# A loop of small matmuls on TensorE during the modulation, and the first gate load as one transfer

## The chip, the core and the metric

The kernel runs on one core of a Trainium2 chip. Its time is the device time of that core in microseconds (us), and less is better. All input weights and caches lie in HBM and are read once.

## What is computed

The reference is one decode step of a transformer block with adaptive layer norm, for 8 sequences of one token, in bf16, cut here to what matters:

```python
mod = (silu(c) @ w_mod).reshape(8, 6, 1, 1024)          # six modulation vectors
sa, ca, ga, sb, cb, gb = (mod[:, i] for i in range(6))
h = layernorm(x) * (1 + ca) + sa
q = h @ wq                                              # 32 heads of 128
p = softmax(q @ k_cache.T * 128 ** -0.5)                # 4 kv heads, 8192 keys each
x = x + ga * ((p @ v_cache) @ wo)
h = layernorm(x) * (1 + cb) + sb
gate, up = h @ W_gate, h @ W_up                         # 1024 to 3584
x = x + gb * ((relu(gate) * up) @ W_down)
```

`w_mod` is 1024 x 6144, `k_cache` and `v_cache` are 8 x 4 x 8192 x 128. With the weights that is 185.6 MB to read.

## The kernel before

Every operation is first entered in a graph (`g.op`), which adds a wait for each read or write that another engine has to finish first; each engine then runs its own list in the order in which it was entered. All matmuls go through the helpers `mm` (line 304) and `tr` (line 308, a transpose), all VectorE operations through line 312, and ScalarE's through line 315. These helpers are the lines that the profile names.

**The stream.** All weights and caches come through one buffer, `ring`, of 11 x 8192 bf16 columns on 128 partitions. The list `stream` fixes the order of the blocks: four of `w_mod` (3 MB each), four of `wq` (2 MB), then the k and v blocks of the 32 pairs of sequence and kv head (2 MB each, `k` ahead of `v` by two), four of `wo` among them, then gate and up in turns (four of each, 1.75 MB), and five of `W_down`, the last two of 0.5 MB. SyncE's queue (SP) issues all of these loads (line 630). A load waits only for the last matmul that used the piece of the ring which it overwrites. `pieces()` says how many transfers a block is cut into: one for all blocks but `("gate", 0)`, which goes as eleven: its second half of 3584 columns, columns 256 to 3583 of its first half, and the first 256 columns in nine transfers of 1, 2, 3, 4, 5, 6, 7, 4 and 96 partitions.

**The stages.** The modulation is a loop of eight `k` over four blocks, with 12 matmuls of 512 columns in each `k`:

```python
for k in range(KD):
    w = place[("mod", k // 2)][:, k % 2, :]
    for f in range(12):
        j, q = f // 4, f % 4
        mm(mbank[j][0][32 * q:32 * q + B, :], siluT[:, k, :], w[:, 512 * f:512 * (f + 1)], ...)
```

Its three PSUM banks are copied out, transposed and added up to `modT`, and `hT` is made of it. The matmuls with `wq` follow (64 of them, on `hT`), then q is laid out, and the attention loop begins: for each of the 32 pairs 64 transposes of the k block on TensorE, copies of them by VectorE and ScalarE, scores, softmax and the product with v, with the stages of three pairs interleaved. After the last pair come the second layer norm, gate and up (112 matmuls with `ring,h2T`), eight transposes, `W_down` (112 matmuls with `ring,hmT`), two VectorE operations and the output's four small transfers.

Of the kernel before, what the change touches and what calls it, by code (L numbers as in the profile page):

```python
# [124 lines left out]
def bass_adaLN_cond__gqa_block_cached__glu_gated_reglu__decode_kernel(  # L125
# [14 lines left out]
    B, _, D = A_x.shape  # L140
    _, G, Sk, Dh = A_k_cache.shape
# [3 lines left out]
    F = B_W_gate.shape[1]  # L145
# [15 lines left out]
    with ExitStack() as es:  # L161
        E = es.enter_context

        def sb(name, shape, dtype):
            return E(nc.sbuf_tensor(name, shape, dtype))
# [6 lines left out]
        identb = sb("identb", [128, 128], bf16)  # L172
# [51 lines left out]
        T = lambda i: PS[:, 2 + i, :]  # L224
# [4 lines left out]
        pT = [("ps", 2), ("ps", 3), ("ps", 4)]  # L229
# [47 lines left out]

        def pieces(key, src):
            d = place[key]
            if key == ("gate", 0):  # L280
                cuts = (0, 1, 3, 6, 10, 15, 21, 28, 32, 128)
                return [(d[:, 1, :], src[:, 1, :]), (d[:, 0, 256:F], src[:, 0, 256:F])] + \
                       [(d[a:z, 0, 0:256], src[a:z, 0, 0:256]) for a, z in zip(cuts[:-1], cuts[1:])]
            return [(d, src)]

        users = {}
        for i, (key, cols, src, shape) in enumerate(stream):
            o = _Op("sp", None, 0)
            o.sem = rsem[i % NSEM]
            landed[i % NSEM] += 16 * len(pieces(key, src))  # L290
            o.semval = landed[i % NSEM]
            loads[key] = o

        def pe(fn, reads=(), writes=(), block=None, deps=()):
            deps = list(deps)
            if block is not None:
                deps.append(loads[block])
            o = g.op("pe", fn, reads, writes, deps)
            if block is not None:
                users[block] = o  # L300
            return o

        def mm(out_, lhsT, rhs, start, stop, reads, writes, block=None, deps=()):
            return pe(lambda e: e.matmul(out_, lhsT, rhs, start=start, stop=stop, skip_group_check=True),  # L304
                      reads, writes, block, deps)
# [66 lines left out]
        layernorm(xT, "xT")  # L372


        mbank = [(S(0), pS[0]), (S(1), pS[1]), (T(0), pT[0])]
        for k in range(KD):
            w = place[("mod", k // 2)][:, k % 2, :]
            for f in range(12):
                j, q = f // 4, f % 4
                mm(mbank[j][0][32 * q:32 * q + B, :], siluT[:, k, :], w[:, 512 * f:512 * (f + 1)], k == 0, k == KD - 1,  # L380
                   ["siluT"], [mbank[j][1]], ("mod", k // 2))
# [6 lines left out]
        for j in range(3):  # L388
            t, key = tbank[j]
# [238 lines left out]
        for i, (key, cols, src, shape) in enumerate(stream):  # L628
            o = loads[key]
            o.fn = (lambda e, o=o, p=pieces(key, src): [e.dma_start(dst, s_).then_inc(o.sem, 16) for dst, s_ in p])  # L630
            o.deps = [users[k] for k in behind[i]]
            head.append(o)
# [41 lines left out]
```

## Time and profile before

| | us |
|---|---|
| time, median of 3 runs | 445.6 (445.5 to 445.78) |
| the profiled execution's own time | 445.82 |
| its span, from the first to the last instruction | 444.0 |

| resource | busy us | share of the span |
|---|---|---|
| TensorE matmuls (4096) | 330.1 | 74% |
| TensorE weight loads (4096) | 205.8 | 46% |
| VectorE | 186.6 | 42% |
| ScalarE | 180.4 | 41% |
| GpSimd | 2.3 | 1% |
| the 16 DMA engines, SP's queue | | 98.3% |

186.25 MB are moved in 15065 packets, a mean of 419 GB/s. The mean granted TensorE clock is 0.88 of full speed. A matmul's busy time overlaps that of its neighbours, so TensorE's 74% doesn't mean that it has only a quarter of the time left, or that it has that much.

### The profile page before, as it was taken

How to read it: one execution, taken by the hardware profiler on the slowest of the kernel's cores; microseconds unless marked ns; L12 is line 12 of the kernel's file. 1: busy time of each engine (PE TensorE's matmuls, PEld its weight loads, DVE VectorE, ACT ScalarE, POOL GpSimd, SP SyncE). 2: the span in 40 equal slices, each digit the busy share in tenths (PEclk: the TensorE clock that was granted, in tenths of full speed). 3: DMA queues.
4: the chain of work that ended last, by engine and by line, in shares of the span. 5: the costliest groups of instructions: out<-in, count | busy, mean ns of one | idle time of the engine just before them, and what ended most of it. 6: DMA issues, size and time to landing. Idle time of an engine off the chain costs nothing.

```text
span 444.0 us, 9316 instructions
## 1 busy us (share of the span) xinstructions
PE 330.1 (74%) x4096; PEld 205.8 (46%) x4096; DVE 186.6 (42%) x491; ACT 180.4 (41%) x235; POOL 2.3 (1%) x11
## 2 busy tenths in 40 slices
PE   1526477988787959988987699888858988755454
PEld 1103065655555636655654466555535655422121
DVE  4002045554454544554554355345543654434010
ACT  3000036755554533744754266465533654420000
POOL 2000000000000000000000000000000000000000
PEclk9996569999998897998998899899987999975955
DMA  8999999999999999999999999999999999999993
GB/s 351 430 418 428 430 432 431 429 427 429 430 432 427 430 429 431 430 431 425 431 430 428 430 428 428 432 430 427 433 424 434 430 426 433 416 421 427 426 427 151
DMA packets 15065, 186.25 MB, mean 419 GB/s; under 512 B 1536, under 2 KB 1696, under 8 KB 4016
## 3 DMA queue, kind: packets, MB, share of 16 engines
q1 hardware_dynamic: 14960, 185.61, 98.3%
q8 instruction: 32, 0.52, 0.4%
q10 hardware_dynamic: 64, 0.04, 0.0%
q14 instruction: 9, 0.07, 0.0%
HBM read 185.63 MB, written 0.02 MB: 418 GB/s over the span
## 4 chain that ended last, share of the span: by engine, by line
DMA 73%; PE 18%; DVE 4%; SPq 3%; ACT 1%; issue 1%; ACTq 0%
DMA ring<-in_A_k_cache_dram 59%; PE PS L308 9%; DMA ring<-in_A_wq_dram 9%; PE PS L304 8%; DMA ring<-in_B_W_down_dram 5%; SPq L630 3%; DVE ov L312 1%; DVE pt L312 1%; ACT ov L315 0%; DVE KT L312 0%; DVE lh L312 0%; ACT KT L315 0%; DVE stat L312 0%; ACT pr L315 0%; DVE yR L312 0%
## 5 line engine op out<-in xcount | busy, mean ns | idle before, releaser
L315 ACT ACTIVATE KT<-PS 128x1024 bf16<-128x1024 bf16 (+1 forms) x132 | 133.2, 1010 | 216.6 <-PE PS L308 107.8
L308 PE MATMUL PS<-identb,ring 128*128 128x128 bf16 x2048 | 154.7, 226 | 37.4 <-DMA ring<-in_A_k_cache_dram 37.3
L308 PEld LDWEIGHTS PS<-identb,ring 128*128 128x128 bf16 x2048 | 125.8, 102 | 63.4 <-DMA ring<-in_A_k_cache_dram 49.4
L312 DVE COPY KT<-PS 128x1024 bf16<-128x1024 bf16 (+1 forms) x130 | 89.6, 690 | 137.3 <-PE PS L308 114.1
L304 PE MATMUL PS<-KT,qz 128*32 128x512 bf16 x512 | 53.0, 401 | 0.4 <-ACT KT L315 0.4
L304 PE MATMUL PS<-ring,pt 128*32 128x512 bf16 x512 | 50.9, 392 | 0.0
L312 DVE TENSOR_REDUCE mp<-PS 128x1 f32<-128x512 f32 x32 | 22.1, 692 | 9.5 <-PE PS L304 6.5
L308 PE MATMUL PS<-identf,ov 128*128 128x128 f32 x128 | 24.2, 318 | 1.5 <-ACT ov L315 1.4
L315 ACT ACTIVATE pr<-PS,nb 128x512 bf16<-128x512 f32 x32 | 22.0, 687 | 5.5 <-DVE nb L312 3.4
L312 DVE COPY pt<-PS 128x512 bf16<-128x512 bf16 x32 | 13.5, 423 | 22.0 <-PE PS L308 22.0
L304 PE MATMUL PS<-ring,siluT 128*8 128x512 bf16 x96 | 10.9, 625 | 14.2 <-DMA ring<-in_w_mod_dram 14.2
L315 ACT ACTIVATE ov<-PS 128x512 f32<-128x512 f32 x32 | 19.0, 592 | 3.6 <-PE PS L304 3.6
L308 PEld LDWEIGHTS PS<-identf,ov 128*128 128x128 f32 x128 | 15.5, 157 | 10.6 <-issue 6.2
L304 PEld LDWEIGHTS PS<-KT,qz 128*32 128x32 bf16 x512 | 13.3, 93 | 14.8 <-issue 1.2
L304 PE MATMUL PS<-lh,onesf 128*128 128x8 f32 x64 | 12.4, 266 | 6.2 <-DVE lh L312 5.9
L304 PE MATMUL PS<-ring,h2T 128*8 128x512 bf16 x112 | 10.3, 475 | 9.0 <-DMA ring<-in_B_W_up_dram 4.5
L304 PEld LDWEIGHTS PS<-ring,pt 128*32 128x32 bf16 x512 | 13.4, 95 | 6.5 <-issue 6.3
L304 PEld LDWEIGHTS PS<-nm,rsel 8*128 8x128 f32 x64 | 9.4, 182 | 13.8 <-DVE nm L312 12.9
L304 PEld LDWEIGHTS PS<-lh,onesf 128*128 128x128 f32 x64 | 9.5, 188 | 11.7 <-DVE lh L312 11.7
L308 PEld LDWEIGHTS PS<-identb,pr 128*128 128x128 bf16 x128 | 7.2, 98 | 15.3 <-ACT pr L315 14.0
L308 PE MATMUL PS<-identb,pr 128*128 128x128 bf16 x128 | 12.7, 222 | 2.0 <-ACT pr L315 2.0
L304 PE MATMUL PS<-ring,hT 128*8 128x512 bf16 x64 | 6.7, 560 | 9.3 <-DMA ring<-in_A_wq_dram 7.9
(88 smaller groups left out, 165.9 us busy)
## 6 DMA issues: line engine op xcount, KB each, us to landing
ring<-in_A_k_cache_dram SPq DMA_DIRECT2D x32, 2048.0 KB, 44.2
ring<-in_A_v_cache_dram SPq DMA_DIRECT2D x32, 2048.0 KB, 41.1
ring<-in_w_mod_dram SPq DMA_DIRECT2D x4, 3072.0 KB, 20.2
ring<-in_A_wq_dram SPq DMA_DIRECT2D x4, 2048.0 KB, 44.5
ring<-in_A_wo_dram SPq DMA_DIRECT2D x4, 2048.0 KB, 45.0
ring<-in_B_W_up_dram SPq DMA_DIRECT2D x4, 1792.0 KB, 29.7
ring<-in_B_W_down_dram SPq DMA_DIRECT2D x3, 2048.0 KB, 29.8
ring<-in_B_W_gate_dram SPq DMA_DIRECT2D x3, 1792.0 KB, 28.1
```

Of the source, the lines that this page charges most:

```text
L304: return pe(lambda e: e.matmul(out_, lhsT, rhs, start=start, stop=stop, skip_group_check=True), reads, writes, block, deps)
L308: return pe(lambda e: e.matmul(out_, in_, ident, start=True, stop=True, is_transpose=True), reads, writes, block)
L312: return g.op("dve", lambda e: getattr(e, name)(*args, **kw), reads, writes)
L315: return g.op("act", lambda e: e.activation(*args, **kw), reads, writes)
L630: o.fn = (lambda e, o=o, p=pieces(key, src): [e.dma_start(dst, s_).then_inc(o.sem, 16) for dst, s_ in p])
```

## The change

TensorE gets a new operation between the modulation's `k` = 2 and `k` = 3. It is a hardware loop (`Fori`) of two turns over a body of 200 matmuls, and one more matmul behind the loop. Each multiplies 32 columns of the bf16 identity (the weights) by one column of it, into a corner of PSUM bank `T(2)` that is overwritten later. Its results are not used. On TensorE's list the loop appears as a branch into the body, the body, an addition to a register and a comparing branch. On the SP list the eleven transfers of `("gate", 0)` become one of 128 x 2 x 3584; nothing else moves on any engine's list.

```diff
         def pieces(key, src):
             d = place[key]
-            if key == ("gate", 0):
-                cuts = (0, 1, 3, 6, 10, 15, 21, 28, 32, 128)
-                return [(d[:, 1, :], src[:, 1, :]), (d[:, 0, 256:F], src[:, 0, 256:F])] + \
-                       [(d[a:z, 0, 0:256], src[a:z, 0, 0:256]) for a, z in zip(cuts[:-1], cuts[1:])]
             return [(d, src)]
...
+        def turns(e):
+            with e.Fori(0, 2):
+                for _ in range(200):
+                    ins = e.matmul(T(2)[0:32, 0:1], identb[:, 0:32], identb[:, 0:1], start=True, stop=True, skip_group_check=True)
+            return e.matmul(T(2)[0:32, 0:1], identb[:, 0:32], identb[:, 0:1], start=True, stop=True, skip_group_check=True)
...
         for k in range(KD):
             w = place[("mod", k // 2)][:, k % 2, :]
+            if k == 3:
+                pe(turns, ["identb"], [pT[2]])
             for f in range(12):
```

## The prediction

> **What bounds the kernel now.** I first read the page's slices, DMA queues and chain.
>
> ```profile
> DMA  8999999999999999999999999999999999999993
> GB/s 351 430 418 428 430 432 431 429 427 429 430 432 427 430 429 431 430 431 425 431 430 428 430 428 428 432 430 427 433 424 434 430 426 433 416 421 427 426 427 151
> q1 hardware_dynamic: 14960, 185.61, 98.3%
> q8 instruction: 32, 0.52, 0.4%
> DMA 73%; PE 18%; DVE 4%; SPq 3%; ACT 1%; issue 1%; ACTq 0%
> ```
>
> The 16 DMA engines are full in every slice but the last. So the end is the end of the stream, plus a tail of 444.0 - 439.8 = 4.2 us (last matmuls, two VectorE operations, output). A TensorE delay costs nothing unless it leaves the DMA engines without orders, or shifts that tail.
>
> The row q8 matters here. 32 packets of 16,384 bytes are 524,288 bytes, exactly 64 bytes for each of the 4096 matmuls and 4096 weight loads: q8 is TensorE's own program, 256 instructions to a packet, and it uses the engines that carry the data. What that does is in the last microseconds, in the busy time by stretches (the last two columns are DMA share and GB/s):
>
> ```profile
> 432.00:433.00 1.00, 0.30 (x8) 0.23 (x12) 0.00 (x0) 0.00 (x0) 0.00 (x0) 0.50 1.00 418
> 433.00:434.00 1.00, 1.00 (x28) 0.63 (x23) 0.00 (x0) 0.00 (x0) 0.00 (x0) 0.50 0.91 381
> 434.00:435.00 1.00, 0.58 (x12) 0.08 (x4) 0.00 (x0) 0.00 (x0) 0.00 (x0) 0.50 0.70 295
> 435.00:436.00 1.00, 0.00 (x0) 0.00 (x0) 0.00 (x0) 0.00 (x0) 0.00 (x0) 0.50 0.58 246
> 437.00:438.00 1.00, 0.40 (x12) 0.26 (x16) 0.00 (x0) 0.00 (x0) 0.00 (x0) 0.50 0.56 217
> 438.00:439.00 1.00, 1.00 (x24) 0.68 (x20) 0.00 (x0) 0.00 (x0) 0.00 (x0) 0.50 0.51 209
> 439.00:440.00 1.00, 0.91 (x20) 0.28 (x8) 0.00 (x0) 0.00 (x0) 0.00 (x0) 0.50 0.14 57
> ```
>
> All engines have the same data, yet six end at 433.5 to 434.4 us, two at 436.2 and 438.1, and eight (the 0.51) run alone until 439.16 to 439.76. The trace's packet records say why: the end marks of the transfers let one follow each engine's lateness, and at each q8 packet one engine falls back by 1.41 us (most of these steps lie between 1.40 and 1.42). The same engine is hit by every eighth packet. So 32 packets are four on each of eight engines: 4 x 1.41 = 5.6 us, the 439.2 - 433.6 seen. **The kernel ends with the engines that fetch TensorE's program.**
>
> **The gate load.** From the queue's rows:
>
> ```profile
> 354.31 7.83 SPq L630 DMA_DIRECT2D ring<-in_B_W_gate_dram  x11
> 362.18 3.53 SPq L630 DMA_DIRECT2D ring<-in_B_W_up_dram  x1
> 365.75 9.02 SPq L630 DMA_DIRECT2D ring<-in_B_W_gate_dram  x1
> ```
>
> Eleven issues take 7.83 us, but one gate issue further on takes 9.02: SP is held because the DMA queues are full (an issue that is not held takes 0.33 to 0.43). So the ten issues that go save SP nothing that counts. On the engines, by the packet records, 128 packets of 512 B follow each other at 23.6 ns, and a 7168 B packet (268 ns) replaces a 6656 B one (about 249.5). An engine with no small piece has before 8 x 249.5 + 6 x 23.6 + two marks of 6 = 2150 ns, after 8 x 268 = 2144: nothing. The engines that take pieces of few partitions have up to 14 small packets and nine marks, and save up to 0.3 us; the records show these mostly early, and of the eight late ones at most one has a single extra piece. Taken: 0, bounds -0.3 and +0.05 us. It hides behind the late engines; if these took the pieces, 0.3 us would show.
>
> **The loop on TensorE's path.** 401 matmuls with 401 weight loads. Rows:
>
> ```profile
> 7.91 0.87 PE L308 MATMUL PS<-identb,KT 8*128 8x8 bf16 x16 [7.91 <-DMA KT<-in_A_x_dram]
> 18.07 2.73 PE L304 MATMUL PS<-ring,siluT 128*8 128x512 bf16 x24 [4.00 <-DMA ring<-in_w_mod_dram]
> 53.23 1.88 PE L304 MATMUL PS<-ring,hT 128*8 128x512 bf16 x16 [3.02 <-DMA ring<-in_A_wq_dram]
> 59.77 3.34 PE L308 MATMUL PS<-identb,ring 128*128 128x128 bf16 x32
> 92.64 1.07 PE L308 MATMUL PS<-identb,ring 128*128 128x128 bf16 x16 [1.60 <-DMA ring<-in_A_k_cache_dram]
> ```
>
> The first eight of the 8-column matmuls start 27 ns apart; the 128-column ones run at 107 ns on the half clock (3.34 us for 32) and 56 on the full one. So the loop takes 401 x 27 = 10.8 us to 401 x 104 = 41.7 us. I take 30 ns, 12 us, since one column is nearest to the 8-column row. [...]
>
> Behind it on TensorE wait k = 3 to 7, 60 matmuls at 0.107 = 6.4 us, and 4.2 us from the last one to `hT` (36.4 to 40.5 now). `wq`'s four groups need 4 x 1.88 = 7.5 us and now end at 55.1, held by their loads. They still do if `hT` is there by 47.6, so if the loop ends by 47.6 - 10.6 = 37.0. Taken: no delay. Beyond that, the attention starts late one for one, but it catches up: the queue's rows show SP released every 8.3 us per pair from 65.8 to 91, while a pair's 4.2 MB at 430 GB/s takes 9.76, so TensorE gains 1.4 us per pair, and first waits for k at 92.64. Ten microseconds are regained in seven pairs, with 44 us between issue and landing in hand.
>
> Starving is the danger: the queue holds orders up to the second k block (its issue row begins at 13.39 and lasts to 34.0), which is 25.2 MB, 58.5 us at 430 GB/s, so until about 60 us. The first v load waits for k = 3, 1.3 us behind the loop, and needs about 1.1 us to its first packet (0.73 to 1.80 at the start). So nothing is lost while the loop ends by 57, a loop of 37.6 us.
>
> **The loop's own program.** This is the term that counts. The static program grows by 402 instructions and about four of control, from some 8250 (32.2 packets) to 8654 (33.8): one packet more, surely, at the boundary at 8448, about 100 matmuls ahead of the end, when all eight engines are still busy. The body starts near instruction 123 and ends near 523, so it spans three packets' instructions. [...] With 33 to 40 packets the fullest engine has five instead of four: its end moves from between 439.16 and 439.76 to between 440.57 and 441.17, so the stream's end moves by 0.81 to 1.41. With five of eight engines hit, 1.2.
>
> [...]
>
> **Sum.** Loop on the path 0, gate 0, fetching +1.2: 445.82 + 1.2 = 447.0 for an execution like the profiled one, which is 0.22 above the median; so **446.8 us** for the median.
>
> **The rivals.**
> [...]
> [...]
> - *Not slower: the added packets miss the late engines.* If after a jump packets go to other engines, which are up to 5.5 us ahead, nothing moves, and only 0 to -0.3 of the gate remains: 445.3 to 445.6. It takes all added packets to miss the late eight. Against it: every eighth packet hit the same engine throughout.
> - [...] Its chance is 0.03, within the last rival's 0.16.
>
> **How the numbers follow.** Forecast 0.62; six packets 0.14; dry stream 0.08; not slower 0.16. 0.2% is 0.9 us, about what a measurement of this kernel can tell from no change. The forecast's own range is 446.4 to 447.0; a small part of it (0.04) lies under 446.5. Slower: 0.58 + 0.14 + 0.08, less 0.04 kept for a gain that no row shows = 0.76. Same: 0.04 + 0.15 of the 0.16 = 0.19. Faster: 0.04 + 0.01 = 0.05. Leaving out both the dry stream and the not-slower case would be over 2 in 10, so the range takes in the latter: 445.4 to 448.5.
>
> **What would show it.** Right: q8 with 33 to 40 packets (37 is my count); the stretches after 433 us with a share near 0.5 until 440 and a last one to 441; still 434 for the early engines; no gap in the DMA slices; `wq`'s last group still ending near 55. Wrong: 41 packets or more; a loop that ends after 57 us with a hole in the slices near 60; a stream that still ends at 439.8.

## The result and the profile after

The kernel with the change takes 446.9 us (median of 12 runs, 446.6 to 447.58) against 445.7 us before (12 runs in the same rounds, 445.5 to 446.0). The ratio is 1.0028, with an interval of 1.0021 to 1.0036: slower by 1.2 us, and a ratio of 1 lies outside the interval. The profiled execution took 446.93 us, with a span of 445.1.

The page of the kernel with the change, slices and queues:

```profile
DMA  8999999999999999999999999999999999999992
GB/s 354 426 414 428 435 430 431 426 428 431 426 431 434 423 432 428 427 434 428 427 430 430 427 427 433 430 424 431 432 428 430 428 431 426 421 427 425 428 418 118
q1 hardware_dynamic: 14768, 185.61, 98.0%
q8 instruction: 34, 0.56, 0.4%
```

The DMA engines are still full from the second slice to the last but one, so nothing ran dry. q8, TensorE's own program, has 34 packets where it had 32. By the trace's packet records 33 of them start ahead of the stream's end and the last one at 442.88, behind it.

The last microseconds of the kernel with the change, busy time by stretches (PE, PEld, DVE, ACT, POOL, then TensorE's clock, DMA share and GB/s):

```profile
433.00:434.00 1.00, 0.10 (x4) 0.10 (x8) 0.00 (x0) 0.00 (x0) 0.00 (x0) 0.50 0.87 365
437.00:438.00 1.00, 0.00 (x0) 0.00 (x0) 0.00 (x0) 0.00 (x0) 0.00 (x0) 0.50 0.59 242
438.00:439.00 1.00, 0.26 (x8) 0.19 (x12) 0.00 (x0) 0.00 (x0) 0.00 (x0) 0.50 0.50 205
439.00:440.00 1.00, 1.00 (x28) 0.63 (x24) 0.00 (x0) 0.00 (x0) 0.00 (x0) 0.50 0.17 70
440.00:441.00 1.00, 1.00 (x20) 0.40 (x12) 0.00 (x0) 0.00 (x0) 0.00 (x0) 0.50 0.05 20
```

Until 439 the picture is that of before: half of the 16 engines still run. The new thing is the last line. A share of 0.05 is one engine of 16, alone until 440.82. With eight engines taken in turn, 33 packets give one of them a fifth packet, and this is that engine. (A packet record doesn't name its engine. What tells the engines apart is the end mark, a record of 4 B with which each engine ends its share of a transfer: the other seven late engines have their last marks by 439.57.) The stream's last data was at 439.76 before and is at 440.82 now, 1.06 us later; the tail behind it is as long as before (4.3 us).

What happens on TensorE, in its timeline:

```profile
18.06 1.45 PE L300 MATMUL PS<-ring,siluT 128*8 128x512 bf16 x12 [3.81 <-DMA ring<-in_w_mod_dram]
19.30 4.61 PE L374 MATMUL PS<-identb 128*32 128x1 bf16 x166
26.00 6.35 PE L374 MATMUL PS<-identb 128*32 128x1 bf16 x233 [2.09 <-issue]
32.27 5.37 PE L300 MATMUL PS<-ring,siluT 128*8 128x512 bf16 x57
53.37 1.88 PE L300 MATMUL PS<-ring,hT 128*8 128x512 bf16 x16 [2.98 <-DMA ring<-in_A_wq_dram]
```

The 401 matmuls run from 19.3 to 32.2 us, 26.7 ns apart, with one gap of 2.1 us in the first turn, from 23.9 to 26.0 us; a q8 packet starts at 23.73 and takes 0.96 us. `wq`'s last group still waits for its load and ends at 55.25, 0.14 us later than before. The loop is off the path.

And the gate load, in the queue's own timeline:

```profile
354.67 0.38 SPq L635 DMA_DIRECT2D ring<-in_B_W_gate_dram  x1
355.44 1.34 SPq L635 DMA_DIRECT2D ring<-in_B_W_up_dram  x1
363.02 2.87 SPq L635 DMA_DIRECT2D ring<-in_B_W_gate_dram  x1
365.95 8.46 SPq L635 DMA_DIRECT2D ring<-in_B_W_up_dram  x1
378.12 12.03 SPq L635 DMA_DIRECT2D ring<-in_B_W_up_dram  x1
390.19 3.99 SPq L635 DMA_DIRECT2D ring<-in_B_W_gate_dram  x1
```

The issue of 7.83 us became one of 0.38, and SP gets some 9 us ahead: the second `up` block is issued at 365.95 where it was at 374.81. It is then held in two issues of 8.46 and 12.03 us, and the last gate block is issued at 390.19, where it was at 390.41. The time saved is time that SP waits.

### The profile page after: what moved, and what is told of

Read it like the earlier page. It is cut to its first block, busy times and chain, and to the rows that moved or that the text cites. A ratio compares the mean times of both kernels' runs of the same rounds, so it can differ in the third digit from the quotient of the medians.

```text
span 445.1 us, 10113 instructions
## 1 busy us (share of the span) xinstructions
PE 342.3 (77%) x4497; PEld 218.2 (49%) x4497; DVE 186.5 (42%) x491; ACT 180.5 (41%) x235; POOL 2.3 (1%) x11
## 3 DMA queue, kind: packets, MB, share of 16 engines
q1 hardware_dynamic: 14768, 185.61, 98.0%
## 4 chain that ended last, share of the span: by engine, by line
DMA 75%; PE 17%; DVE 4%; SPq 2%; ACT 1%; issue 1%; ACTq 0%
DMA ring<-in_A_k_cache_dram 58%; DMA ring<-in_A_wq_dram 11%; PE PS L304 9%; PE PS L300 8%; DMA ring<-in_B_W_down_dram 6%; SPq L635 2%; DVE ov L308 1%; DVE pt L308 1%; DVE qz L308 0%; ACT ov L311 0%; DVE KT L308 0%; ACT KT L311 0%; DVE lh L308 0%; DVE stat L308 0%; ACT pr L311 0%
## 5 line engine op out<-in xcount | busy, mean ns | idle before, releaser
L304 PE MATMUL PS<-identb,ring 128*128 128x128 bf16 x2048 | 156.8, 228 | 35.0 <-DMA ring<-in_A_k_cache_dram 35.0
L304 PEld LDWEIGHTS PS<-identb,ring 128*128 128x128 bf16 x2048 | 127.4, 103 | 61.8 <-DMA ring<-in_A_k_cache_dram 46.1
L300 PE MATMUL PS<-KT,qz 128*32 128x512 bf16 x512 | 53.9, 408 | 0.4 <-ACT KT L311 0.4
L304 PE MATMUL PS<-identf,ov 128*128 128x128 f32 x128 | 25.1, 328 | 1.5 <-ACT ov L311 1.4
L300 PE MATMUL PS<-ring,h2T 128*8 128x512 bf16 x112 | 11.3, 516 | 5.7 <-DMA ring<-in_B_W_up_dram 3.7
L300 PE MATMUL PS<-ring,hmT 128*8 128x256 bf16 x112 | 5.8, 372 | 9.1 <-DMA ring<-in_B_W_down_dram 9.0
```

Source lines behind the costliest of these rows:

```text
L304: return pe(lambda e: e.matmul(out_, in_, ident, start=True, stop=True, is_transpose=True), reads, writes, block)
```

## The experiments

The theory: the stream ends with the DMA engine that took most packets of TensorE's program, and each packet costs its engine 1.41 us. Since packets go to eight engines in turn, only the count on the fullest engine matters. The rivals: the loop's time in the modulation, the jump, the gate load, or a fixed price for each packet. The edits are shortened. They are shown against the kernel with the change; in the runs that say "no loop" the loop is left out too, and the last run's edit is shown against the kernel before.

**The loop alone** (the eleven gate transfers are kept).

```diff
         def pieces(key, src):
             d = place[key]
+            if key == ("gate", 0): ...   # as before
```

> The loop alone; the first gate load keeps its eleven transfers. Theory (the stream ends with the DMA engine that took most packets of TensorE's program, 1.41 us each): 33 packets ahead of the stream's end, one engine with five, +1.2 us, 446.9. Rival (the single gate load costs the time): no change, 445.7.

446.81 us (446.51 to 447.58), ratio 1.0016, interval 0.9996 to 1.0035. The interval, like those of the next three runs, is wide because four of the 33 runs of the kernel before in these rounds read 448.08 to 450.41. The other 29 lie between 445.51 and 445.85, and all eleven runs of the loop alone lie above them. 33 packets, last data at 440.63.

**The gate load alone.**

```diff
-            if k == 3:
-                pe(turns, ["identb"], [pT[2]])
```

> The single gate load alone, no loop. Theory: 32 packets as before, eight engines with four, 0 (-0.2 to +0.05) us, 445.6; eight engines end together near 439.5. Rival (the single gate load costs the time): 446.9.

445.68 us (445.5 to 445.95), ratio 0.9995, interval 0.9977 to 1.0012. So the 1.2 us is the loop's. The single gate load is worth nothing that can be measured. (In the one profile the stream's last data comes at 439.41, 0.35 us earlier than in that of before, but the medians of the times are equal, 445.68 and 445.67.)

**The same matmuls in a short body.**

```diff
-            with e.Fori(0, 2):
-                for _ in range(200):
+            with e.Fori(0, 40):
+                for _ in range(10):
```

> The whole change, but the same 400 matmuls as forty turns of a body of 10 in place of two turns of 200, so the program grows by some 25 instructions in place of 406 and stays under the next boundary of 256. Theory: 32 packets, 445.6, though TensorE does as much in the modulation and branches 40 times. Rival (TensorE's time in the modulation, or the jumps, cost): 446.9 or more.

445.69 us (445.53 to 445.79), ratio 0.9994, interval 0.9976 to 1.0011. The TensorE timeline and the end of this run:

```profile
19.02 16.56 PE L374 MATMUL PS<-identb 128*32 128x1 bf16 x400
35.48 5.23 PE L300 MATMUL PS<-ring,siluT 128*8 128x512 bf16 x60
53.04 1.88 PE L300 MATMUL PS<-ring,hT 128*8 128x512 bf16 x16 [3.82 <-DMA ring<-in_A_wq_dram]
```
```profile
438.00:439.00 1.00, 1.00 (x28) 0.64 (x24) 0.00 (x0) 0.00 (x0) 0.00 (x0) 0.50 0.53 217
439.00:440.00 1.00, 0.77 (x16) 0.23 (x12) 0.00 (x0) 0.00 (x0) 0.00 (x0) 0.50 0.06 25
440.00:441.00 1.00, 0.46 (x8) 0.00 (x0) 0.46 (x2) 0.00 (x0) 0.00 (x0) 0.50 0.00 0
```

TensorE does the same 401 matmuls and branches 40 times; the loop lasts 3.5 us longer than with the long body, and the kernel loses nothing. 32 packets, and no data moves in the last line of the stretches again.

**The same program length without a loop.**

```diff
-            with e.Fori(0, 2):
-                for _ in range(200):
-                    ins = e.matmul(...)
+            for _ in range(200):
+                ins = e.matmul(...)
```

> The whole change without the loop: the 200 matmuls are executed once, straight on, and the one behind them. The program grows as much, TensorE's work by half as much, and no jump is left. Theory: 33 packets ahead of the stream's end, 446.9. Rival (the second turn's work or the jump back costs): 445.6.

446.88 us (446.64 to 447.81), ratio 1.0008, interval 0.9979 to 1.0037. 33 packets ahead of the stream's end, last data at 440.51. Half the work and no jump, and the time is as with the loop. These two runs, taken in the same rounds, settle it: every one of the eleven straight runs (446.64 or more) lies above every one with the short body (445.79 or less), so the program's length counts, not what TensorE does with it.

**Eight packets more.** In place of the loop, 33 of the small matmuls ahead of each pair's transposes.

```diff
             for j in range(8):
                 if n < N:
+                    if j == 0:
+                        for _ in range(33):
+                            mm(X[0:32, 288:289], identb[:, 0:32], identb[:, 0:1], True, True, ["identb"], [pX])
                     slot_transpose(n, j)
```

> Single gate load, no loop; 33 of the same small matmuls stand ahead of each of the 32 pairs' first transposes (about 0.9 us a pair, less than TensorE's 1.4 us of slack), which makes the program longer by 2112 instructions. Theory (the fullest engine decides): 40 packets, five on each of the eight engines, so only one step of 1.41 us: 447.0, and the eight engines end together near 440.9. Rival (each added packet costs 1.2 us): 8 x 1.2 = 9.6 us, 455.

446.93 us (446.82 to 447.0), ratio 1.0025, interval 1.0017 to 1.0034. Eight packets more cost as much as one more. The stretches of this run:

```profile
438.00:439.00 1.00, 0.28 (x8) 0.21 (x12) 0.00 (x0) 0.00 (x0) 0.00 (x0) 0.50 0.50 205
439.00:440.00 1.00, 1.00 (x28) 0.61 (x24) 0.00 (x0) 0.00 (x0) 0.00 (x0) 0.50 0.51 209
440.00:441.00 1.00, 1.00 (x20) 0.36 (x12) 0.00 (x0) 0.00 (x0) 0.00 (x0) 0.50 0.27 111
```

Where the changed kernel has one engine past 439.6, here all eight run on (0.51 until 440) and end together: their last end marks lie at 440.45 to 440.83, where those of the gate load alone lie at 439.02 to 439.40. That is 1.39 us later in the mean, one packet for each.

**One more on top.** As above, with 39 in place of 33.

> As the run with 33, but with 39 per pair: 2496 instructions more, one packet more than there. Theory: 41 packets ahead of the stream's end, one engine with six: a second step, 448.0 to 448.5, with one engine alone at the end. Rival (the small matmuls' own time delays the end): less than 0.2 us over the run with 33, which has nearly as many.

448.06 us (448.01 to 448.32), ratio 1.005, interval 1.0036 to 1.0065. The second step is there, 1.13 us above the run with 33. The trace has 42 packets, one more than expected; the 42nd starts at 441.09, in the last microsecond of the stream, which ends at 442.03. From 440.87 on one engine alone still moves data, without a break while the 42nd packet comes, so that packet is on another engine, and 41 decide the end:

```profile
440.00:441.00 1.00, 1.00 (x24) 0.63 (x25) 0.00 (x0) 0.00 (x0) 0.00 (x0) 0.50 0.31 127
441.00:442.00 1.00, 1.00 (x24) 0.49 (x16) 0.00 (x0) 0.00 (x0) 0.00 (x0) 0.50 0.13 41
```

**A longer body.** The whole change with 450 in place of 200.

```diff
-                for _ in range(200):
+                for _ in range(450):
```

> The whole change with a body of 450 in place of 200, still two turns: 901 matmuls, some 31 us, until about 50 us, so the attention starts some 13 us late; the program grows by 906 instructions, to 35.8 packets. Theory (a late start is regained, the body stays held, the fullest engine decides): 35 packets ahead of the stream's end, five on three engines, 446.9 to 447.2. Rivals: the late start costs, up to 460; the jump back over four packets fetches them again, 39 or more packets, from 41 on 448.2.

447.16 us (447.11 to 447.71), ratio 1.0037, interval 1.0022 to 1.0052. 35 packets. Three engines end late, at 440.44, 440.74 and 441.06, and the other 13 are done by 439.24: five packets on three engines, as expected. TensorE's timeline:

```profile
19.18 4.61 PE L374 MATMUL PS<-identb 128*32 128x1 bf16 x166
26.28 3.55 PE L374 MATMUL PS<-identb 128*32 128x1 bf16 x128 [2.49 <-issue]
33.02 3.55 PE L374 MATMUL PS<-identb 128*32 128x1 bf16 x128 [3.19 <-issue]
39.22 12.86 PE L374 MATMUL PS<-identb 128*32 128x1 bf16 x477 [2.65 <-issue]
68.41 2.03 PE L304 MATMUL PS<-identb,ring 128*128 128x128 bf16 x32
132.75 1.07 PE L304 MATMUL PS<-identb,ring 128*128 128x128 bf16 x16 [0.75 <-DMA ring<-in_A_k_cache_dram]
```

A group of 128 matmuls is 256 instructions, one packet. In the first turn TensorE stands still for 2.5 to 3.2 us ahead of each of them and ahead of the last 477, which I read as waiting for its program. In these 477, which hold the jump and the whole second turn, there is no gap, and no packet comes between 36.7 and 54.4 us. So the body was still held. (The 35 packets say it too: the program has 35.8, and none came twice.) The attention starts at 68.4 in place of 59.8 us, and TensorE first waits for k at 132.75 in place of 92.64: a late start is regained, and the time is that of five packets on the fullest engine.

**The last load of W_down with rows moved off the late engines.** If eight engines are late by 5.6 us, rows might be given to the others.

```diff
+            if key == ("wd", 4):
+                cuts = (0, 48, 99, 116, 121, 126, 128)
+                return [(d[a:z], src[a:z]) for a, z in zip(cuts[:-1], cuts[1:])]
```

> No loop, single gate load; the last load of W_down (128 rows of 4096 B) goes as six transfers of 48, 51, 17, 5, 5 and 2 partitions, which by the packet records of the kernel before run on 16, 3, 1, 5, 5 and 2 engines from the first one on. Each late engine then moves 3 of its 8 rows of 0.155 us no more, the first engine has 40. Theory (the eight late engines are the bound): the end 0.5 to 0.8 us earlier, 444.9 to 445.2. Rival (the engines are not told apart so, or many transfers cost more than one): 445.7 or more.

(What a late engine loses there are five of eight rows, 0.78 us. The queue's row has 14784 packets, 16 more than the 14768 of the change: end marks of 16 + 3 + 1 + 5 + 5 + 2 = 32 shares in place of 16.) 447.9 us (447.38 to 448.02), ratio 1.0044, interval 1.003 to 1.0057: slower by 2.2 us, where the theory wanted a gain. By the packet records, the 8192 B packets of W_down's 2 MB blocks, which are not cut, have medians of 400 to 467 ns between 433 and 436 us, where they take 309 in the kernel before. From 433 to 435 not one of them takes less than 431. So transfers that are not cut are slowed as well. Two runs looked for the reason.

**Eight transfers of 16 neighbouring partitions.**

```diff
+            if key == ("wd", 4):
+                return [(d[16 * i:16 * (i + 1)], src[16 * i:16 * (i + 1)]) for i in range(8)]
```

> After the run with moved rows. No loop, single gate load; the last load of W_down goes as eight transfers of 16 neighbouring partitions. Each of the 16 DMA engines still moves eight rows of 4096 B, as in one transfer, but all 16 write into the same 16 partitions at a time. Theory (a group of eight partitions takes no more than about one engine's rate, 4096 B in 0.155 us; rows moved to another engine slow the engine whose partitions they are): a transfer of 64 KB into two such groups takes about 1.2 us, eight take 9.7 in place of 1.24, up to 454. Rival (it was the number of transfers or the few engines that cost in that run): 445.7 to 446.

446.97 us (446.69 to 447.17), ratio 1.0029, interval 1.0018 to 1.0041.

**Eight transfers of every eighth partition.**

```diff
+            if key == ("wd", 4):
+                return [(d[i:128:8], src[i:128:8]) for i in range(8)]
```

> As the run with 16 neighbouring partitions, with as many transfers and rows, but each takes every eighth partition, so each engine writes one row into a group of its own. Theory: 445.7 (to 445.9 for the marks of seven more transfers). Rival (the number of transfers costs): as much as the run with neighbouring partitions.

447.31 us (447.0 to 447.64), ratio 1.0036, interval 1.0021 to 1.0051. The theory of the partitions falls: it wanted 454 for the one and 445.7 for the other, and they lose 1.3 and 1.6 us. The rival of the first, 445.7 to 446, falls too; nearest is that of the second, that as many transfers cost about as much. The 8192 B packets take 481 and 548 ns (medians) in the microsecond from 433, and 309 again from 436 on.

**Rows moved 50 us ahead of the end.**

```diff
             if key == ("gate", 0):
-                cuts = (0, 1, 3, 6, 10, 15, 21, 28, 32, 128)
-                return [(d[:, 1, :], src[:, 1, :]), (d[:, 0, 256:F], src[:, 0, 256:F])] + ...
+                cuts = (0, 96, 113, 118, 123, 128)
+                return [(d[:, 1, :], src[:, 1, :])] + [(d[a:z, 0, :], src[a:z, 0, :]) for a, z in zip(cuts[:-1], cuts[1:])]
```

> No loop. Rows are moved as in the run with six transfers of W_down, but 50 us ahead of the end, in the first gate load, where the kernel before had its eleven transfers without a slower packet beside them: its second half is one transfer, its first half goes as 96, 17, 5, 5 and 5 partitions (16, 1, 5, 5 and 5 engines). Each late engine then moves 6 in place of 8 rows of 7168 B (0.268 us each), the first engine 26. Theory (late engines are the bound, and the last runs lost by transfers cut up close to the end): 0.4 to 0.55 us earlier than with one transfer, 445.1 to 445.3. Rival (rows moved to other engines slow the others wherever they stand): 445.7 or more.

451.0 us (450.44 to 451.15), ratio 1.0108, interval 1.0088 to 1.0128: slower by 5.2 us, where the theory wanted a gain again. The slices of this run's page show where:

```profile
GB/s 351 431 423 427 434 430 428 432 424 431 427 432 429 430 428 430 432 426 430 427 429 433 424 436 423 435 424 433 425 432 427 430 430 424 276 345 427 428 426 168
```

In slices 35 and 36, 382 to 404 us, the rate falls to 276 and 345 GB/s. By the packet records 7168 B take about 490 ns in place of 272 from 385 to 397, and not one of them less than 402. In that time 16 busy engines move some 3 MB, three times what the cut transfers hold, so other loads are slowed with them. Why is open: it is not the number alone, since the eleven transfers of the kernel before left the packets beside them at a median of 272 ns, and the two runs above don't put it on the partitions that the transfers write. No version was found that beats the kernel before.

## Why the prediction was right, step by step

- **What bounds the kernel.** Held. That q8 is TensorE's program is borne out by its counts: 2112, 2496 and 906 more instructions brought 8, 10 and 3 more packets. Packets ahead of the stream's end and its last data, from the packet records: 32 at 439.41 to 439.76 (before, gate alone, short body); 33 at 440.51 to 440.82 (the change, loop alone, straight); 35 at 441.06; 40 at 440.83; 42 at 442.03, of which 41 count. The steps are where eight engines in turn put them, between 32 and 33 and between 40 and 41. From 33 to 40 there is no step; the ends differ by up to 0.55 us.
- **The size of the step.** 1.41 us for a packet was right: 1.39 in the mean of the eight engines, from the gate load alone to eight packets more. 0.81 to 1.41 for the end was right too: 1.06 in the two profiles, 1.2 in the medians.
- **How many packets.** Here the working was off, without a consequence. My count was 37; there were 33, what the longer program gives with no packet a second time, and one more behind the end. So one engine was hit, not five of eight, and the end showed it as one engine alone. The count within 33 to 40 matters little, which is what the prediction rested on. But no run shows the five engines hit for which the sum has 1.2, within 0.81 to 1.41: with one, the mean over the eight ends is 1.0, and the profiles show 1.06. That the medians also differ by 1.2 is in this part luck. In the run with the long body, 900 instructions or 3.5 packets, the jump brought no packet and no gap either; no run here has a longer body.
- **The loop on the path.** 30 ns a matmul was near (26.7). TensorE stood still once, for 2.1 us, and not at the jump but in the first turn. The loop ended at 32.2, ahead of the 37.0 up to which no delay was expected. None came, as taken; that a late start would be regained is shown by the long body.
- **The gate load.** 0, as taken: 445.68 against 445.67.
- **The rivals.** Six packets on an engine needed 41, and the change has 33; where a run reached 41 the time was 448.06, 2.4 us above the kernel before. The dry stream needed a loop to 57 us; even the long body's ended at 52. The not-slower case needed packets dealt to other engines, and the order of eight held. Joining small transfers gained nothing (445.68 against 445.67).

## What to carry to other kernels

In a kernel that keeps the DMA engines full, read the DMA share of the last ten microseconds in steps of one: if it stands at a half, as here (0.51 in the microsecond from 438 us of the kernel before), some engines are late, and the question is what they alone carry. Here it is TensorE's unrolled program, 256 instructions to a packet, and adding code costs little (up to 0.4 us between 33 and 40 packets in these runs) until the count of packets passes a multiple of eight, and then 1.2 us (from 32 to 33) or 1.13 (from 40 to 41) at once. Repeated work in a hardware loop with a short body left the number of packets, and so the stream's end, as it was, though the loop itself ran 3.5 us longer on TensorE, which had the time here.

## What the runs showed of the hardware that was not expected

- In the run with the long body, 900 instructions, the loop's second turn brought no packet and no gap, so the body was held. The branch back took 0.24 us in the changed kernel's trace.
- TensorE outran its own program, as I read the gaps: at 26.7 ns a matmul with its weight load, 256 instructions last 3.4 us, and it stood still for 2.1 us once in the changed kernel, 2.8 us once in the straight run, and 2.5, 3.2 and 2.7 us in the first turn of the long body. In the attention of the kernel before, where packets come some 11 us apart, no such gap shows (0.4 us at most).
- Cutting a load into certain sets of smaller transfers also slowed packets of loads that were not cut: 8192 B from 309 ns to medians of up to 548 for two to five microseconds, and 7168 B from 272 to 490 ns for 12 us. The cause is not known.
